# Local and strided scores in shared PSUM pairs, with a new order of operations

## The chip, the cores and the metric

The kernel runs on one core of one Trainium2 chip. The metric is the device time of one execution in microseconds; before the change it was 312.59 us (median of three runs, 310.74 to 312.9).

## The reference

A sparse attention over 8 batches, 8 heads, 576 positions and 64 dimensions per head, and behind it a feed-forward layer with ELU. All inputs and the output are float32.

```python
scores = q @ k^T / sqrt(64)
rel = pos[:, None] - pos[None, :]
mask_local   = (rel >= 0) & (rel < 32)                 # heads 0..3
mask_strided = (rel >= 0) & (pos[None] % 32 == pos[:, None] % 32)   # heads 4..7
attn = softmax(where(mask, scores, -1e9)) @ v
x = attn.transpose(0, 2, 1, 3).reshape(8 * 576, 512)
h = x @ w_in                                           # w_in 512 x 2048
g = where(h > 0, h, exp(min(h, 0)) - 1)
out = g @ w_out                                        # w_out 2048 x 512
```

## The kernel before

**Tokens of a sequence** are taken in 8 classes modulo 8, 72 positions each (`NS`, `RS`). A strided head then needs only positions of its own classes, so its scores are small blocks of 72 by 72; a local head needs, for each window of 96 positions (`LQ`), 128 keys. Heads are worked on in pairs: a key such as `3s1` is batch 3, strided (`s`) or local (`l`), pair 1 (`y`). Each pair is done in two halves (`u`).

**Attention, one half of a pair**: `S` computes the scores into two PSUM banks of 288 columns each (`scores`, L464: six local or eight strided matmuls of 64 rows, alternating between the banks), `e` takes the exp on ScalarE for both banks at once (`exp_s`, L471, 576 elements per partition), `m` multiplies by the 0/1 mask on VectorE (`mask`, L478 and L484), `O` multiplies by v and by ones, which gives the output and the sums of the exps (`pv`, L527 strided, L534 local; batches 0 and 1 in an older form with 64-column matmuls), `n` and `r` take Ln and Exp(-) of the sums on ScalarE (L562, L568), and `x` writes the product into `xT` (L593). Batches 0 to 2 are loaded plainly and transposed on TensorE (`T`, L418 and L421) with copies out of PSUM on VectorE (`c`) or ScalarE (`C`); for batches 3 to 7 the transposition is a DMA on SP's queue (`X`).

**Feed-forward**: 9 chunks of 512 tokens. Layer 1 has 16 blocks `m` per chunk, each four matmuls of 512 columns (`L`; in chunk 0 as `a`, inputs 2 and 3, the strided heads, and `b`, inputs 0 and 1, the local heads; L623). `h` is the exp of h on ScalarE (L631), `i` clamps it on VectorE (L640) or `j` on ScalarE (L638), `g` takes the maximum with h on VectorE (L651, after `j` L649). Layer 2 has four blocks `kk` of 128 tokens, each in four parts of four matmuls (`Z`, L657). `o` (ScalarE) or `q` (VectorE) copies a block to SBUF (L663) into one of four rotating `osb` tiles, and `t` stores it in two or three pieces from SP's queue (L675). The very last block is done in two halves of 256 columns (`Y`, L683, and `y`: the second half is copied by ScalarE and VectorE and stored by SP and ScalarE).

**Loads** (`D`) are issued by POOL: q, k, v by class (`qs`, `ks`, `ql`, ...; with two heads per load for batch 0), `wi0` to `wi3` and `wj0` for w_in (`wi0` and `wj0` half a quarter each) and `wo0` to `wo3` for w_out. The q and k of the first strided pair of batch 0 come by SP and ScalarE's queues into a staging tile. The other loads of batch 0 stand in the program ahead of the order. `V` copies the v rows that two windows share; `W` copies the strided v into a layout with ones between.

**What sets the order**: the string `ORDER`. It is gone through token by token, and each engine's queue is the sub-sequence of the tokens that it executes; PSUM banks are the digits at the end of a token (`S.3s0.1.56` uses banks 5 and 6). Semaphores keep readers behind writers, and a writer of a bank or of a rotating tile behind its last reader, a store's landing included. Within one engine nothing overtakes.

```python
    for tok in ORDER.split():
        f, *a = tok.split(".")
        run[f](*a)
```

Of the kernel before, what the change touches and what calls it, by code (L numbers as in the profile page):

```python
# [9 lines left out]
BF16 = mybir.dt.bfloat16  # L10
I32 = mybir.dt.int32
ALU = mybir.AluOpType
# [3 lines left out]
S = 576  # L16
D = 64
# [19 lines left out]
T.0s0.k.0.1 S.0s0.0.12 c.0s0.k.1 T.0s0.q.3.1 e.0s0.0 c.0s0.q.1 S.0s0.1.67 m.0s0.0 T.0s1.q.0 e.0s0.1  # L37
O.0s0.0.12 c.0s1.q m.0s0.1 T.0s1.k.7 n.0s0.0 F.ml D.wi0.0 O.0s0.1.56 r.0s0.0 c.0s1.k x.0s0.0 D.wj0.0
n.0s0.1 S.0s1.0.34 r.0s0.1 T.0l0.q.7 D.wi1.0 e.0s1.0 x.0s0.1 S.0s1.1.01 c.0l0.q T.0l0.k.2 e.0s1.1
D.wi2.0 m.0s1.0 c.0l0.k O.0s1.0.67 D.wi3.0 m.0s1.1 n.0s1.0 S.0l0.0.01 S.0l0.1.23 D.qs.1 V.0.0  # L40
e.0l0.0 O.0s1.1.45 e.0l0.1 D.ks.1 m.0l0.0 T.0l1.k.0 r.0s1.0 m.0l0.1 O.0l0.0.23 n.0s1.1 x.0s1.0
# [3 lines left out]
b.0.0 h.0.4 b.0.2 h.0.0 i.0.4 a.0.5.7 D.wo0.0 h.0.2 a.0.6.3 i.0.0 g.0.4 b.0.6 j.0.2 b.0.5 g.0.0  # L45
h.0.6 a.0.11.6 h.0.5 g.0.2 b.0.11 j.0.6 a.0.8.4 i.0.5 D.wo1.0 h.0.11 b.0.1 g.0.5 a.0.9.5 h.0.1 g.0.6
b.0.8 j.0.11 D.wo2.0 i.0.1 b.0.9 h.0.8 g.0.1 a.0.7.7 h.0.9 a.0.14.3 i.0.8 T.1s0.q.0 g.0.11 j.0.9
D.wo3.0 b.0.7 g.0.8 T.1s1.q.2 h.0.7 a.0.3.6 c.1s1.q T.1s0.k.1 C.1s0.q a.0.15.4 g.0.9 D.qs.2 C.1s0.k
T.1s1.k.2 i.0.7 b.0.15 c.1s1.k S.1s0.1.01 h.0.15 g.0.7 b.0.3 D.ks.2 e.1s0.1 b.0.14 i.0.15 h.0.3
g.0.15 T.1l1.q.7 S.1s0.0.01 h.0.14 m.1s0.1 S.1s1.0.45 D.ql.2 e.1s0.0 i.0.3 a.0.12.2 i.0.14 b.0.12  # L50
e.1s1.0 m.1s0.0 T.1l0.q.0 g.0.14 h.0.12 T.1l0.k.1 O.1s0.0.45 D.kl.2 C.1l0.q m.1s1.0 a.0.10.3 i.0.12
n.1s0.0 g.0.3 T.1l1.k.0 r.1s0.0 b.0.10 C.1l1.k x.1s0.0 a.0.13.6 g.0.12 h.0.10 O.1s0.1.45 C.1l0.k
c.1l1.q b.0.13 D.vs.2 V.1 n.1s0.1 S.1l1.0.12 h.0.13 Z.0.2.0.7 i.0.10 e.1l1.0 g.0.10 Z.0.1.0.0
r.1s0.1 m.1l1.0 j.0.13 x.1s0.1 S.1l0.1.12 g.0.13 O.1l1.0.34 D.vl.2 e.1l0.1 Z.0.2.1.7 n.1l1.0 m.1l0.1
r.1l1.0 Z.0.1.1.0 x.1l1.0 S.1l0.0.12 S.1s1.1.34 S.1l1.1.56 e.1l0.0 Z.0.2.2.7 e.1l1.1 m.1l0.0
Z.0.1.2.0 e.1s1.1 m.1l1.1 O.1l1.1.56 O.1l0.0.34 n.1l1.1 O.1s1.0.12 n.1l0.0 Z.0.2.3.7 m.1s1.1 n.1s1.0
r.1l0.0 r.1l1.1 Z.0.1.3.0 x.1l0.0 o.0.2 x.1l1.1 r.1s1.0 Z.0.0.0.3 t.0.2 o.0.1 x.1s1.0 Z.0.0.1.3
t.0.1 Z.0.0.2.3 Z.0.0.3.3 O.1s1.1.12 o.0.0 O.1l0.1.67 n.1s1.1 T.2s1.q.0 t.0.0 T.2s1.k.3 n.1l0.1
c.2s1.q r.1s1.1 T.2l0.k.5 c.2s1.k T.2l0.q.4 r.1l0.1 T.2l1.k.0 x.1s1.1 C.2l0.k T.2l1.q.3 x.1l0.1
S.2s1.0.12 C.2l1.k W.2 T.2s0.q.5 L.1.13.6 e.2s1.0 D.qs.3 c.2s0.q C.2l1.q c.2l0.q T.2s0.k.7 m.2s1.0  # L60
L.1.6.5 h.1.13 D.ks.3 V.2 j.1.13 c.2s0.k L.1.11.4 D.vs.3 h.1.6 g.1.13 D.ql.3 S.2s0.0.23 i.1.6 h.1.11
S.2l0.1.01 L.1.10.6 g.1.6 e.2s0.0 X.qs.3 i.1.11 e.2l0.1 L.1.8.7 m.2s0.0 h.1.10 g.1.11 O.2s0.0.01
h.1.8 L.1.5.2 m.2l0.1 i.1.10 n.2s0.0 i.1.8 O.2s1.0.34 X.ks.3 Z.0.3.0.5 g.1.10 r.2s0.0 g.1.8 h.1.5
Z.0.3.1.5 x.2s0.0 n.2s1.0 L.1.4.7 r.2s1.0 i.1.5 D.kl.3 g.1.5 L.1.7.6 h.1.4 x.2s1.0 Z.0.3.2.5 h.1.7
i.1.4 L.1.1.4 i.1.7 g.1.4 L.1.0.3 g.1.7 h.1.1 i.1.1 L.1.12.7 h.1.0 g.1.1 D.vl.3 X.ql.3 L.1.2.6 i.1.0
h.1.12 g.1.0 L.1.14.4 h.1.2 i.1.12 g.1.12 j.1.2 L.1.15.3 D.qs.4 h.1.14 g.1.2 L.1.3.7 h.1.15 i.1.14
g.1.14 j.1.15 S.2l1.1.12 Z.0.3.3.5 e.2l1.1 X.kl.3 g.1.15 h.1.3 m.2l1.1 S.2l1.0.01 S.2s0.1.23 o.0.3
L.1.9.4 i.1.3 e.2s0.1 g.1.3 D.ks.4 t.0.3 O.2l1.1.56 e.2l1.0 m.2s0.1 Z.1.0.0.7 h.1.9 m.2l1.0 n.2l1.1
# [84 lines left out]
def kernel(  # L153
# [597 lines left out]
```

## Time and profile before

| What | Value |
|---|---|
| runs | 312.59, 310.74, 312.9 us |
| profiled execution: span | 309.4 us (no separate time is listed for it) |
| TensorE busy | 297.2 us, 96% |
| ScalarE busy | 233.7 us, 76% |
| VectorE busy | 223.4 us, 72% |
| POOL busy | 74.8 us, 24% |
| granted TensorE clock, mean | 0.977 |
| first layer-1 matmul | at 18.38 us |
| first layer-2 matmul | at 39.44 us |
| end of the last matmul | 305.47 us |

How to read it: the span goes from the first to the last instruction of the profiled execution. Busy is the union of an engine's instructions; matmuls are pipelined, so a row's mean duration (381 ns for a 512-column matmul) is longer than the distance between two starts (216 ns). A row of a group reads: line, engine, operation, tiles, shapes, number of instructions, busy time, mean duration of one, and behind the bar the engine's idle time ahead of them and what ended it. "issue" is time in which the engine waited for nothing that the profile shows. The clock is a share of full speed, by slices of 7.7 us in the head of the page.

### The profile page before, as it was taken

Reading aid. Unit: us, or ns where it says so; the run is one execution under the profiler, and the core shown is the slowest. Engines: PE = TensorE matmul, PEld = TensorE weight load, DVE = VectorE, ACT = ScalarE, POOL = GpSimd, SP = SyncE. Lnnn points to the kernel's source line nnn. Section 1 sums busy time; section 2 is a strip of 40 time slices with the busy share of each in tenths; the row PEclk is TensorE's granted clock in tenths of the full one; section 3 lists DMA queues with packets and bytes.
Section 4 is the critical chain, followed back from the end, with each engine's and each line's share of the span. In section 5 each row is a group of like instructions: output and inputs, shape, how many; then the busy total and the mean of one; then the engine's idle time right before and its main releaser. Section 6 shows DMA issues by size and latency. Waiting matters only on the chain.

```text
span 309.4 us, 6379 instructions
## 1 busy us (share of the span) xinstructions
PE 297.2 (96%) x2374; PEld 151.6 (49%) x2412; DVE 223.4 (72%) x445; ACT 233.7 (76%) x410; POOL 74.8 (24%) x104
## 2 busy tenths in 40 slices
PE   5989999999999999999999999999999999999994
PEld 5754545544554455444544544455444544444443
DVE  6869972999669976898689679946798359990100
ACT  4769976979887899887998997879886767881211
POOL 8933310761084048003810082000000000000000
PEclk9559999999999999999999999999999999999999
DMA  8999999999999999994999589222200220002222
GB/s 161 189 206 206 195 206 213 165 133 152 151 200 161 123 201 183 106 125 87 190 155 122 119 113 159 47 67 71 68 3 0 70 68 1 0 2 57 67 79 70
DMA packets 96952, 36.29 MB, mean 117 GB/s; under 512 B 77754, under 2 KB 92442, under 8 KB 96922
## 3 DMA queue, kind: packets, MB, share of 16 engines
q0 software_dynamic: 64608, 19.40, 61.0%
q1 hardware_dynamic: 31878, 16.09, 28.9%
q10 hardware_dynamic: 436, 0.40, 0.5%
q8 instruction: 19, 0.31, 0.4%
q14 instruction: 11, 0.09, 0.1%
HBM read 39.41 MB, written 9.44 MB: 158 GB/s over the span
## 4 chain that ended last, share of the span: by engine, by line
PE 72%; DVE 15%; DMA 6%; issue 4%; ACT 2%; DVEq 0%; ACTq 0%
PE ps L657 34%; PE ps L623 27%; DVE g L651 6%; DMA vl<-in_v_dram 5%; DVE he L640 5%; PE ps L464 3%; PE ps L527 2%; PE ps L534 2%; DVE xT L593 1%; DMA g<-in_k_dram 1%; DVE g L649 1%; PE ps L683 1%; PE ps L421 1%; PE ps L418 1%; ACT he L631 1%
## 5 line engine op out<-in xcount | busy, mean ns | idle before, releaser
L623 PE MATMUL ps<-xT,w_in_sb 128*128 128x512 bf16 x560 | 129.6, 381 | 1.5 <-DVE g L651 0.4
L657 PE MATMUL ps<-w_out_sb,g 128*128 128x512 bf16 x538 | 128.9, 379 | 1.8 <-issue 1.0
L631 ACT ACTIVATE he<-ps 128x512 f32<-128x512 f32 x144 | 84.5, 594 | 23.3 <-PE ps L623 21.0
L623 PEld LDWEIGHTS <-w_in_sb 128*128 128x128 bf16 x576 | 55.1, 98 | 65.3 <-issue 2.3
L657 PEld LDWEIGHTS <-g 128*128 128x128 bf16 x560 | 50.6, 98 | 53.4
L651 DVE TENSOR_TENSOR g<-he,ps 128x512 bf16<-128x512 bf16 x112 | 74.0, 681 | 1.5
L640 DVE TENSOR_SCALAR he<-he 128x512 bf16<-128x512 f32 x112 | 46.3, 431 | 16.2 <-ACT he L631 15.7
L593 DVE TENSOR_TENSOR xT<-ps,ln 64x576 bf16<-64x576 f32 (+1 forms) x64 | 42.4, 678 | 21.6 <-ACT ln L568 21.1
L471 ACT ACTIVATE e<-ps 128x576 bf16<-128x576 f32 (+1 forms) x64 | 39.4, 646 | 5.8 <-PE ps L464 5.0
L562 ACT ACTIVATE ln<-ps 64x576 f32<-64x576 f32 (+1 forms) x64 | 36.3, 584 | 5.8 <-PE ps L527 2.6
L568 ACT ACTIVATE ln<-ln 64x576 f32<-64x576 f32 (+1 forms) x64 | 38.7, 620 | 1.4
L663 ACT COPY osb<-ps 128x512 f32<-128x512 f32 x27 | 15.8, 585 | 29.1 <-PE ps L657 26.1
L232 POOL DMA_DIRECT2D vs<-in_v_dram x8 | 5.3, 662 | 71.7 <-DVE vsp L603 69.4
L478 DVE TENSOR_TENSOR pm<-e,mask_s 72x576 bf16<-72x576 bf16 x32 | 14.4, 451 | 11.3 <-ACT e L471 10.8
L649 DVE SCALAR_TENSOR_TENSOR g<-he,ps 128x512 bf16<-128x512 bf16 x32 | 21.7, 680 | 0.6
L638 ACT ACTIVATE he<-he 128x512 bf16<-128x512 f32 x32 | 20.1, 627 | 0.7
L484 DVE TENSOR_TENSOR pm<-e,mask_l 128x576 bf16<-128x576 bf16 x32 | 14.5, 456 | 5.4 <-ACT e L471 4.4
L238 POOL DMA_DIRECT2D ql<-in_q_dram x20 | 16.3, 821 | 0.5 <-issue 0.4
L245 POOL DMA_DIRECT2D kl<-in_k_dram x20 | 15.5, 801 | 1.2 <-DMA vs<-in_v_dram 0.9
L527 PEld LDWEIGHTS <-vsp 72*128 72x128 bf16 x192 | 9.1, 98 | 5.8 <-DVE vsp L603 0.7
L700 DVE COPY osb<-ps 128x128 f32<-128x128 f32 x1 | 0.3, 291 | 15.0 <-ACT osb L699 15.0
L534 PEld LDWEIGHTS <-vl 128*128 128x128 bf16 x144 | 8.2, 97 | 4.4
(87 smaller groups left out, 176.4 us busy)
## 6 DMA issues: line engine op xcount, KB each, us to landing
out_dram<-osb SPq DMA_DIRECT2D x31, 144.0 KB
w_out_sb<-in_moe_w_out_dram POOLq DMA_DIRECT2D x4, 512.0 KB, 15.4
vl<-in_v_dram POOLq DMA_DIRECT2D x7, 288.0 KB, 6.6
qs<-in_q_dram POOLq DMA_DIRECT2D x5, 320.0 KB, 9.5
ks<-in_k_dram POOLq DMA_DIRECT2D x5, 320.0 KB, 11.2
vs<-in_v_dram POOLq DMA_DIRECT2D x5, 320.0 KB, 6.0
w_in_sb<-in_moe_w_in_dram POOLq DMA_DIRECT2D x3, 512.0 KB, 11.2
ql<-in_q_dram POOLq DMA_DIRECT2D x20, 72.0 KB, 6.9
```

What stands on the lines that cost most here:

```text
L238: nc.gpsimd.dma_start(out=t[0:RS, h % 2, :, h // 2, :], in_=q[b, h].rearrange("(p s) d -> p s d", s=NS))
L471: nc.scalar.activation(e[0:R], tiles.pop(("S", key, u))[0:R], ACT.Exp, scale=scale)
L562: nc.scalar.activation(t, s_ps, ACT.Ln)
L568: nc.scalar.activation(t, t, ACT.Exp, scale=-1.0)
L593: nc.vector.tensor_mul(dst, o_ps, rc)
L623: nc.tensor.matmul(tiles["h", ch, m], lhsT=w_in_sb[:, c, m * 128:(m + 1) * 128], rhs=xT[:, c, ch * CHUNK:(ch + 1) * CHUNK], start=(c == 2) ...
L631: nc.scalar.activation(e, tiles["h", i[0], i[1]], ACT.Exp)
L638: nc.scalar.activation(e1, e, ACT.Relu, bias=1.0, scale=-1.0)
L640: eng.tensor_scalar(e1, e, scalar1=1.0, scalar2=1.0, op0=ALU.min, op1=ALU.subtract)
L649: nc.vector.scalar_tensor_tensor(dst, e1, -1.0, h, op0=ALU.mult, op1=ALU.max)
L651: nc.vector.tensor_tensor(dst, e1, h, op=ALU.max)
L657: nc.tensor.matmul(ops, lhsT=g[ch % 2][:, m, kk * 128:(kk + 1) * 128], rhs=w_out_sb[:, m, :], start=(m == 0), stop=(m == MC - 1), skip_gro ...
```

## The change

For batches 3 to 7 the scores of a half of a local pair and three of the four strided blocks of a half of a strided pair share a pair of banks of 504 columns (`PW`: 288 local, 3 x 72 strided). The fourth strided blocks of all four halves share one pair of banks of 288 columns (`j` = 4). So a batch has five tokens `P`, five exps and five masks, where it had eight of each. The mask comes from one tile `mask_x` with the strided mask three times behind the local one. `O` picks its parts from these tiles; the masked tiles live until both local and strided `O` have read them. The loads of batch 0 and two mask selects become tokens of the order, and the whole order is made anew: sequence, banks, which clamps are `i` or `j` (112 and 32 before, 87 and 57 after), which output copies are `o` or `q` (27 and 8 before, 16 and 19 after), and the places of the loads, transposing DMAs and stores. Of the order, the beginning up to the first layer-1 tokens, one packed stretch and the end are shown.

```diff
+PACK = (3, 4, 5, 6, 7)
+PW = W + 3 * RS
...
-w.7.28 F.k1 F.vs k.k.0 k.q.0 T.0s0.k.0.0 F.ms C.0s0.k.0 T.0s0.q.1.0 K.q.1 k.k.1 c.0s0.q.0
...
-D.vs.1 T.0l1.q.1 r.0s1.1 c.0l1.k O.0l0.1.67 n.0l0.0 r.0l0.0 c.0l1.q n.0l0.1 V.0.1 D.ql.1 S.0l1.1.01
-x.0l0.0 r.0l0.1 x.0s1.1 e.0l1.1 S.0l1.0.23 x.0l0.1 a.0.0.4 e.0l1.0 m.0l1.1 D.kl.1 O.0l1.1.67 m.0l1.0
-O.0l1.0.23 n.0l1.1 r.0l1.1 a.0.2.5 n.0l1.0 x.0l1.1 a.0.1.0 r.0l1.0 D.vl.1 x.0l1.0 a.0.4.6 b.0.4
...
-Z.8.0.2.1 Z.8.0.3.1 Z.8.1.0.0 o.8.0 Z.8.1.1.0 t.8.0 Z.8.1.2.0 Z.8.1.3.0 o.8.1 t.8.1 Y.8.3.0.1
-y.8.3.0 Y.8.3.1.2 y.8.3.1
+F.k1 D.qs1.0 D.ks1.0 F.ms w.7.28 k.k.0 T.0s0.k.0.0 K.q.1 k.q.0 T.0s0.q.3.0 T.0s0.q.7.1 F.vs
+T.0s1.q.6 T.0s1.k.1 k.k.1 D.vs0.0 T.0s0.k.5.1 c.0s0.q.0 c.0s1.q c.0s1.k C.0s0.k.0 C.0s0.q.1
+S.0s0.0.67 e.0s0.0 D.ql0.0 D.kl0.0 S.0s1.0.01 D.vl0.0 F.m1 c.0s0.k.1 S.0s0.1.23 D.vs1.0 e.0s1.0
...
+F.ml e.0l0.1 e.0l0.0 O.0s1.0.01 V.0.0 m.0l0.1 r.0s0.1 T.0l1.q.3 D.ks.1 c.0l1.q n.0s1.0 O.0l0.1.67
+x.0s0.1 C.0l1.k O.0s1.1.23 r.0s1.0 n.0l0.1 D.qs.1 S.0l1.1.45 x.0s1.0 T.1s0.k.0 r.0l0.1 T.1s0.q.1
+n.0s1.1 r.0s1.1 x.0l0.1 T.1s1.q.7 e.0l1.1 C.1s0.k x.0s1.1 c.1s0.q m.0l0.0 m.0l1.1 D.vl1.0 S.0l1.0.23
+V.0.1 D.wi1.0 S.1s0.0.01 e.0l1.0 m.0l1.0 D.qs.2 O.0l0.0.56 D.wi2.0 e.1s0.0 m.1s0.0 O.0l1.1.34
+n.0l0.0 n.0l1.1 O.0l1.0.01 a.0.7.2 r.0l0.0 x.0l0.0 a.0.4.5 r.0l1.1 x.0l1.1 T.1s1.k.6 a.0.5.3 D.wi0.0
+c.1s1.q D.vs.1 n.0l1.0 r.0l1.0 x.0l1.0 b.0.5 b.0.7 D.wi3.0 h.0.7 c.1s1.k i.0.7 S.1s0.1.67 b.0.4
...
+P.3.3.12 e.3p.3 t.1.1 P.3.4.34 D.qs.5 L.2.0.0 e.3p.2 h.2.0 m.3p.3 L.2.8.7 h.2.8 L.2.6.1 e.3p.4
...
+L.8.13.1 h.8.13 i.8.13 g.8.13 Z.8.1.0.4 q.7.1 Z.8.1.1.4 Z.8.2.2.0 t.7.2 Z.8.2.3.0 Z.8.1.2.4
+Z.8.1.3.4 Y.8.3.0.5 t.7.3 Z.8.0.1.6 Z.8.0.2.6 t.7.1 q.8.1 Z.8.0.3.6 q.8.2 t.8.2 q.7.0 t.7.0 t.8.1
+y.8.3.0 q.8.0 t.8.0 Y.8.3.1.7 y.8.3.1
...
+    p_pm4 = ctx.enter_context(tc.tile_pool(name="p_pm4", bufs=2)) if PACK else None
...
-    mask_l = consts.tile([128, 2, NS, 3, LN], BF16, tag="mask_l", name="mask_l")
+    mask_x = consts.tile([128, 2, PW if PACK else W], BF16, tag="mask_x", name="mask_x")
+    mask_l = mask_x[:, :, 0:W].rearrange("p u (s b n) -> p u s b n", s=NS, b=3)
...
+        elif b == 0:
+            y = int(what[2])
+            if nm == "vl":
+                load_vpair(0, y)
+            else:
+                load_runs(nm, 0, 2 * y, 2)
...
-    load_runs("vs", 0, 0, 2)
-    load_runs("qs", 0, 2, 2)
-    load_runs("ks", 0, 2, 2)
-    load_runs("vs", 0, 2, 2)
...
-    for y in range(2):
-        load_runs("ql", 0, 2 * y, 2)
-        load_runs("kl", 0, 2 * y, 2)
-        load_vpair(0, y)
...
+        elif what == "mx":
+            mx = mask_x[:, :, W:]
+            nc.vector.memset(mx, 0.0)
+            for u in range(2):
+                nc.vector.tensor_copy(mx[0:RS, u].rearrange("p (i n) -> p i n", n=RS),
+                                      mask_s.unsqueeze(1).to_broadcast([RS, 3, RS]))
...
+    def scores_packed(b, j, bk):
+        i0, i1, j = int(bk[0]), int(bk[1]), int(j)
+        sc = tiles["S", b + "p", j] = ps[:, i0:i1 + 1:i1 - i0, 0:PW if j < 4 else W]
+        items = ([("l", j // 2, j % 2, i) for i in range(3)] + [("s", j // 2, j % 2, i) for i in range(3)]
+                 if j < 4 else [("s", k // 2, k % 2, 3) for k in range(4)])
+        c0 = 0 if j == 4 else W
+        for c, y, u, i in items:
+            P = Pair(f"{b}{c}{y}")
+            for z in range(2):
...
+                nc.tensor.matmul(dst, lhsT=P.kT[pr, k0:k0 + 128], rhs=rhs, start=True, stop=True,
+                                 skip_group_check=True)
+            if P.str:
+                c0 += RS
+
+    def exp_packed(key, j):
+        j = int(j)
+        R, n = (128, PW) if j < 4 else (RS, W)
+        e = tiles["e", key, j] = p_e.tile([128, 2, PW], BF16, tag="e", name="e")
+        nc.scalar.activation(e[0:R, :, 0:n], tiles.pop(("S", key, j))[0:R], ACT.Exp, scale=scale)
+
+    def mask_packed(key, j):
...
+            pm = p_pm.tile([128, 2, PW], BF16, tag="pm", name="pm")
+            nc.vector.tensor_mul(pm, e, mask_x[:, j % 2].unsqueeze(1).to_broadcast([128, 2, PW]))
+        tiles["pm", key, j] = pm
...
+        def part(z, i):
+            if not P.str:
+                return local_cols(pm[:, z, 0:W], i)
+            if P.b in PACK and i == 3:
+                return pm4[:, z, k * RS:(k + 1) * RS]
+            return pm[0:RS, z, c0 + i * RS:c0 + (i + 1) * RS]
```

More of the change, by code (lines that the diff above doesn't have):

```diff
@@ L541, in pv @@
         P, u = Pair(key), int(u)
-        pm = tiles.pop(("pm", key, u))
+        if P.b in PACK:
+            k = 2 * P.y + u
+            pm, pm4 = (tiles["pm", key[0] + "p", i] for i in (k, 4)) if P.str else (
+                tiles["pm", key[0] + "p", k], None)
+            c0 = W
+        else:
+            pm, c0 = tiles.pop(("pm", key, u)), 0
+        def part(z, i):
[4 more added lines that the diff above has]
+            return pm[0:RS, z, c0 + i * RS:c0 + (i + 1) * RS]
         if not P.old:
             ov = banks(bk)
-            pv_new(P, pm, u, ov)
+            pv_new(P, part, u, ov)
             ys = slice(P.y * D, (P.y + 1) * D)
@@ L706 @@
         "f": lambda *a: fill(*a, nc.scalar.copy),
+        "P": scores_packed,
         "c": lambda *a: copy_T(nc.vector.tensor_copy, *a),
         "C": lambda *a: copy_T(nc.scalar.copy, *a),
[L709 removed]
+        "S": scores, "O": pv,
+        "e": lambda key, u: (exp_packed if key[1] == "p" else exp_s)(key, u),
+        "m": lambda key, u: (mask_packed if key[1] == "p" else mask)(key, u), "n": log_sums, "r": recip, "x": write_x,
         "V": copy_vloc, "W": copy_vstr, "D": load, "X": dma_T,
```

256 lines of the change are left out of this document (134 added, 122 removed).

## The prediction

> **What bounds the kernel now.** I read the page's head first, then engine time by stretch, the costliest groups, the list of waits, and last the timelines of the start and the end.
>
> ```profile
> span 309.4 us, 6379 instructions
> PE 297.2 (96%) x2374; PEld 151.6 (49%) x2412; DVE 223.4 (72%) x445; ACT 233.7 (76%) x410; POOL 74.8 (24%) x104
> ...
> PEclk9559999999999999999999999999999999999999
> ```
>
> TensorE is busy nearly always; only slices 2 and 3 show half the clock. The same by stretch (columns: length; busy time of PE, weight load, DVE, ACT, POOL; clock; DMA share; GB/s):
>
> ```profile
> 0.00:20.44 20.44, 15.77 (x254) 12.71 (x255) 15.38 (x50) 13.36 (x27) 14.84 (x28) 0.70 1.23 183
> 20.44:40.00 19.56, 19.15 (x210) 9.65 (x212) 16.81 (x36) 17.19 (x35) 7.37 (x10) 0.96 1.36 201
> 40.00:290.00 250.00, 246.90 (x1829) 120.89 (x1861) 190.11 (x358) 200.21 (x344) 52.58 (x66) 1.00 0.90 108
> ...
> 305.47:309.40 3.93, 0.00 (x0) 0.00 (x0) 0.29 (x1) 0.27 (x1) 0.00 (x0) 0.92 0.16 49
> ```
>
> From 40 to 290 us TensorE idles 3.1 us in all. Whatever the change does to ScalarE and VectorE there, it cannot win more than these 3.1 us plus what it takes out of TensorE's own stream. What else can move is the start (until the chunks flow) and the last 3.93 us, in which no matmul runs.
>
> **The packed scores, counted.** Per batch 3 to 7, eight score blocks of two banks by 288 columns become four of 504 (local 288 plus three strided blocks of 72) and one of 288. The matmuls stay: 24 local and 32 strided before, 4 x 12 + 8 after. Exps and masks fall from 8 to 5.
>
> ```profile
> L471 ACT ACTIVATE e<-ps 128x576 bf16<-128x576 f32 x32 | 20.1, 647 | 3.0 <-PE ps L464 2.5
> L562 ACT ACTIVATE ln<-ps 64x576 f32<-64x576 f32 x48 | 30.0, 642 | 3.5 <-PE ps L527 2.6 <-PE ps L534 0.2
> L562 ACT ACTIVATE ln<-ps 128x288 f32<-128x288 f32 x16 | 6.2, 411 | 2.3 <-PE ps L507 1.2 <-PE ps L491 1.1
> L484 DVE TENSOR_TENSOR pm<-e,mask_l 128x576 bf16<-128x576 bf16 x32 | 14.5, 456 | 5.4 <-ACT e L471 4.4
> ```
>
> No row has 1008 elements. From 411 ns at 288 and 642 at 576, an element costs 0.80 ns and an instruction 180; so 1008 elements take about 0.99 us, and a batch's exps 4 x 0.99 + 0.65 = 4.6 instead of 5.2 us: 2.7 us of ScalarE for five batches. Bounds: one instruction no cheaper than 0.65, no dearer than the two that it replaces, 1.29; at 1.29 ScalarE gains nothing. VectorE saves about as much, 2 us, by the same reasoning from 456 ns. On the path both are worth nothing while TensorE is full. They are also spent again: the new order moves 25 clamps from VectorE (431 ns) to ScalarE (627) and 11 output copies from ScalarE (585) to VectorE (689), which leaves ScalarE some 6 us heavier.
>
> **Mode changes, the one gain in TensorE's stream.** The list of waits has this line:
>
> ```profile
> PEld L464 <- issue: 12.3, 30, 0.6
> ```
>
> Thirty times the weight load stood still about 0.41 us ahead of scores, waiting for nothing shown. TensorE itself feels less: a 512-column matmul is followed by its like after 216 ns, by scores after 311; and the last score matmul before a full-size one takes about 130 instead of about 40. So each change costs 0.09 us. Counted along both orders, changes between 128-row, 64-row and 64-column matmuls fall from 92 to 74: **-1.6 us** (bounds -0.9 if only leaving or entering costs, -2.2). The Trainium skill, TensorEngine Tiling, "Key Properties", says that a change of tiling mode drains TensorE; the row agrees, and it speaks for this part.
>
> **The body of the order.** By TensorE time between tokens (0.216 us per 512-column matmul), a layer-1 bank is reused after 4.9 us (median) where it was 3.5, and from scores to their PV in batches 3 to 7 lie 13.9 us (least 3.8) where it was 3.2 (least 1.5). Exp, mask and the queue ahead of them hide easily. Against that stands one stretch, some 165 to 180 us along TensorE's work, where ScalarE's work back to back (0.49 us an exp of h, 0.54 a clamp, 0.93 a packed exp) is 1.1 times TensorE's: up to 1.5 us of delay; the longer bank reuse covers most. For loads, each first packed block of a batch has its transposing DMA at least some 10 us earlier, though it now needs local and strided operands together. I take **+0.3** (bounds -2 and +3).
>
> **The start.** Loads land in order of issue: half loads of 160 KB at 6.60, 7.38, 8.23, then every 0.8 to 0.9 us; 320 KB in 1.6, 1 MB of weights (512 KB here) in 2.5. The new queue puts q and k of the second strided pair first, and ahead of the last v half and the first weights it puts k and q of batch 1. By these steps the last v half lands at 17.4 (14.17 before), w_in's second quarter at 19.9; chunk 0 now starts there, with m = 7, 4, 5. That would do, since the first layer-1 matmul ran at 18.38. But TensorE's queue also has batch 1's three strided transposes (0.62 us each at half clock) ahead of the scores 0l1.0, and all the rest of batch 0 hangs on those. Walking the three queues with the rows: first exp 8.8 (VectorE fills vs_p, 0.95 us, ahead of the first copy; it was 7.46); S.0l1.1 at 17.4 (17.14 before); transposes 17.9 to 19.7; S.0l1.0 at 19.8 (18.02); its exp to 20.5 and mask to 21.4, behind V.0.1; PV until 22.8; Ln, Exp and product until 24.35. So layer 1 can go on with inputs 0 and 1 at 24.4, where it did at 22.08. In TensorE work at warm prices, 14.9 us are then done against 14.4, so the start is **+2.0** behind. Cover: the batch 1 work pulled ahead is not lost, it is in the 14.9. Two edits cost nothing: the two mask selects on POOL (0.33 and 0.31 us) now stand between batch 0's loads, but POOL issues a load in 0.6 us while one lands in 0.8, and without that lead each would delay the later landings by its 0.3; the new fill of the joint mask, about 0.8 us on VectorE, falls where VectorE has 15% to spare and nothing in batch 2 reads it.
>
> Then the clock, by the windows in which it was granted:
>
> ```profile
> 8.37:11.79 3.42, 3.42 (x66) 2.76 (x68) 2.58 (x9) 2.71 (x6) 3.35 (x7) 0.50 1.57 189
> 11.79:15.20 3.41, 3.25 (x72) 2.69 (x68) 2.95 (x7) 2.42 (x6) 3.08 (x5) 0.50 1.69 185
> 15.20:18.61 3.41, 2.73 (x52) 2.20 (x48) 3.31 (x9) 3.23 (x10) 1.27 (x2) 0.50 1.29 204
> 18.61:22.03 3.42, 3.06 (x21) 1.44 (x21) 1.81 (x5) 2.11 (x5) 1.18 (x1) 0.50 1.25 208
> 22.03:25.44 3.41, 3.41 (x17) 1.57 (x16) 1.55 (x4) 2.27 (x5) 0.76 (x1) 1.00 1.24 206
> ```
>
> Busy with transposes and small blocks, TensorE stayed at 0.50; full clock came after the window with five 512-column matmuls. In the new order these begin at about 22.8, a window later, so the clock may return at 25.4: six matmuls at 0.43 instead of 0.216 us, +1.3. I take +0.7 between 0 and 1.3: the start is **+2.7** (bounds -1, if the weights' landing alone sets it, and +4). The Trainium skill, TensorE: Matmul & The Clock Gate, "Part 4: PE-mode transpose", says that transposes do not count as busy for the clock; by it the later window is right and the sum would be 0.6 higher. The windows agree as far as they go.
>
> **The end.** Before, each output tile had its store long ahead:
>
> ```profile
> 301.81 3.66 PE L683 MATMUL ps<-w_out_sb,g 128*128 128x256 bf16 x32
> 303.80 0.37 ACT L696 COPY osb<-ps 128x256 f32<-128x256 f32 x1 [1.16 <-PE ps L683]
> 305.50 0.27 ACT L699 COPY osb<-ps 128x128 f32<-128x128 f32 x1 [1.33 <-PE ps L683]
> 305.80 0.29 DVE L700 COPY osb<-ps 128x128 f32<-128x128 f32 x1 [14.96 <-ACT osb L699]
> 306.12 0.65 ACTq L675 DMA_DIRECT2D out_dram<-osb  x1
> ```
>
> After the last matmul (305.47): copies, issue at 306.12, landing at 308.09, end. Four osb tiles rotate. In the new order q.8.0, on VectorE, takes the tile of q.8.1, and t.8.1 stands on SP behind t.8.2 and t.7.0; and y.8.3.1's VectorE copy is queued behind q.8.0, its SP store behind t.8.0. With E the end of the last matmul: q.8.1, q.8.2, q.7.0 until E-4; t.8.2, t.7.0, t.8.1 (three pieces each at 0.37) until E-1.2; t.8.1 lands 1.5 later, E+0.3; q.8.0 until E+1.1; t.8.0 until E+2.2; y.8.3.1's store at E+2.3 to 2.6, where it was E+0.65. That is **+2.2** with landings at 0.2 to 0.5 slower (bounds 0, if the wait does not bind, and +3).
>
> ```profile
> ACT osb L663 <- DMA out_dram<-osb: 2.9, 1, 2.9
> ```
>
> That such a copy does wait for the store of its tile is seen once already.
>
> **Sum**, against the profiled execution's span: 2.7 + 2.2 - 1.6 + 0.3 = **+3.6 us**, 309.4 to 313.0. The three runs lie 1.3 to 3.5 us above that span, median 312.59; so the forecast is **316.2**, 1.2% slower; own range 314.3 to 318.2.
>
> **Rivals.**
> 1. *Not slower: the start fills.* If O.0l1.0 ends by 20 us, layer 1 starts as w_in lands, and batch 1's work already done counts in full: start -1.0, sum -0.1, 312.5. For it: ScalarE is busy 13.36 of 20.44 us, there is room. Against: the transposes at half clock. It decides at a start of layer 1's second half before 21.5 us.
> 2. *The tail does not bind*: +1.4, 314.0. For it: stores end 1.4 us after issue in places; against, VectorE's and SP's order.
> 3. *ScalarE becomes the bound* at 155 to 195 us: the surplus of 1.5 us shows in full and a second stretch near 75 to 90 (0.98) adds 0.8: 318.5. Against: bank reuse of 4.9 us.
> 4. *Faster by over 1%*: rivals 1 and 2 together and 2 us of the 3.1 idle us gone: 308.3.
> 5. *The change does not do what it says*: packed exps at 1.29 us free nothing; ScalarE is then 1.5 us per two batches fuller and rival 3 gets likelier, up to 319.
>
> **Chances.** Forecast 0.47, rival 1 0.18, 2 0.12, 3 0.12, 4 0.05, 5 0.06. A measurement of this kernel tells about 1% (3.1 us) from no change. Slower by over that (above 315.7): 0.33 of the forecast's 0.47, rivals 3 and 5, and 0.04 of 2 with a worse start: 0.55. Faster 0.05; within 1% 0.40. The range runs from rival 1 with a little more to rivals 3 and 5: 311.5 to 320.
>
> **What would show it.** Start: first L471 at about 8.8, second half of layer 1 near 24.4, clock 1.00 from 22.0 or 25.4. Packed: L471's new form of 1008 elements near 0.99 us, x20, and the mask near 0.68. Mode changes: fewer than 30 stops of PEld before scores. Body: TensorE idle at most 4 us between 45 and 290. End: a VectorE copy to osb waiting for a DMA, and some 6 us between the last matmul and the end. I am wrong if layer 1 starts before 20 us, if the end stays at 4 us, or if TensorE has stretches with ScalarE full in the middle.

## The result, and the profile after

The changed kernel takes 313.34 us (median of 13 runs, 312.81 to 315.34), the kernel before 311.83 (13 runs, 310.74 to 313.63): ratio 1.0055, 95% interval 1.0039 to 1.007. So it is slower by 1.5 to 1.7 us, where 3.6 were forecast.

The page's head, and engine time by stretch:

```profile
span 313.5 us, 6289 instructions
PE 300.6 (96%) x2373; PEld 153.9 (49%) x2412; DVE 226.1 (72%) x420; ACT 236.7 (75%) x408; POOL 74.5 (24%) x104
```

```profile
0.00:20.44 20.44, 17.22 (x284) 14.41 (x284) 14.85 (x49) 14.11 (x30) 14.87 (x28) 1.00 1.18 184
20.44:40.00 19.56, 18.25 (x196) 8.79 (x197) 15.20 (x32) 14.13 (x30) 7.50 (x10) 1.00 1.39 200
40.00:290.00 250.00, 246.21 (x1801) 120.73 (x1834) 190.44 (x332) 207.25 (x348) 52.16 (x66) 1.00 0.82 106
309.05:313.50 4.45, 0.00 (x0) 0.00 (x0) 0.29 (x1) 0.27 (x1) 0.00 (x0) 1.00 0.40 119
```

In the middle TensorE idles 3.8 us (3.1 before), ScalarE is busy 7 us more, and 4.45 us lie behind the last matmul (3.93). The clock column reads 1.00 at the start only because records of the clock are missing there; the distance of the matmuls shows half clock until 27.4 us (below).

**Two things about the numbers come first.** Each of the 13 runs lists its time and its span; they differ by 1.66 to 1.81 us. So the execution of before with span 309.4 stands for some 311.1 us, 0.7 under its median, and that of after (313.5, time 315.25) lies 1.9 above its median. The two profiles are 4.1 us apart, the medians 1.5: about 2.5 us of what the profiles show between them belongs to these two executions and not to the kernels.

To see where, I set up an account that doesn't depend on matmul records (38 or 39 are missing in each of these two traces, no weight load is): TensorE's work is every weight load's matmul at its undisturbed price (0.216 us for 512 columns; 288.6 us in all, in both kernels), and the **lag** is the time minus the work done by then.

| us | before | after | difference | forecast |
|---|---|---|---|---|
| lag at 40 us (start) | 10.9 | 13.3 | +2.4 | +2.7 |
| added from 40 us to the last matmul (body) | 6.0 | 7.2 | +1.2 | -1.6 + 0.3 |
| last matmul to end | 4.0 | 4.5 | +0.5 | +2.2 |
| sum | 20.9 | 25.0 | +4.1 | +3.6 |

The sum of the forecast nearly meets that of these two executions, by errors that cancel: that is luck. The row of the body is no accident of the two. From the weight load that runs at 45.2 us in *after* to the end of the last matmul, four traces with this body (*after*, *start_both*, *tail*, *fill_after*, see below) take 263.5 to 263.9 us; from the load at 45.05 us in *before*, three traces with the body of before (*before*, *fill_early*, *fill_all*) take 259.8 to 260.4. (The two stretches hold different work, so only the scatter within each is to be compared.) The new instructions themselves, shapes kept apart:

```profile
L504 ACT ACTIVATE e<-ps 128x1008 bf16<-128x1008 f32 x20 | 19.6, 1006 | 2.5 <-PE ps L495 1.6 <-DVE pm L517 0.9
L517 DVE TENSOR_TENSOR pm<-e,mask_x 128x1008 bf16<-128x1008 bf16 x20 | 13.6, 680 | 5.0 <-ACT e L504 4.8
L504 ACT ACTIVATE e<-ps 72x576 bf16<-72x576 f32 x5 | 3.2, 641 | 1.3 <-PE ps L495 1.3
```

1.006 us for the exp of 1008 elements and 0.68 for its mask, as worked out; the change does what it says. In the list of waits (each line: microseconds in total, times, longest) the stops of the weight load ahead of scores (two lines now) fall from 30 to 23, and those ahead of layer 1, which I read as a bank that isn't free yet, rise; before they were 2.3 us, 9 times:

```profile
PEld L495 <- issue: 5.5, 13, 0.4
PEld L689 <- issue: 5.2, 17, 0.5
PEld L468 <- issue: 4.4, 10, 0.8
```

That second line turned out to be the main one. The end, in order of time:

```profile
304.32 6.02 SPq L741 DMA_DIRECT2D out_dram<-osb  x15
304.75 0.37 ACT L762 COPY osb<-ps 128x256 f32<-128x256 f32 x1 [6.33 <-PE ps L749]
307.34 0.69 DVE L729 COPY osb<-ps 128x512 f32<-128x512 f32 x1 [2.45 <-PE ps L723]
309.38 0.29 DVE L766 COPY osb<-ps 128x128 f32<-128x128 f32 x1 [1.35 <-DMA out_dram<-osb]
309.70 0.57 ACTq L741 DMA_DIRECT2D out_dram<-osb  x1
```

The copy at 307.34 (q.8.0) waited for its own matmuls (PE) and for no store. By the semaphores that it waits on, it took the tile of q.8.2, whose stores are the first three of the 15 (304.32 to 305.43). The stores of q.8.1, whose tile the forecast gave it, were still being issued (306.76 to 307.92) when it began. The last copy, at 309.38, ran right behind ScalarE's (309.08 to 309.35), as before. What remains is SP's queue of 15 issues, which runs until 310.34, 1.3 us past the last matmul. Before, it was 1.0:

```profile
299.21 7.23 SPq L675 DMA_DIRECT2D out_dram<-osb  x9
```

The DMA packets agree. Before, the last packet of the output belongs to ScalarE's store (2.27 us past the last matmul; SP's 2.01); after, to SP's (2.85; ScalarE's 2.68).

### The profile page after: what moved, and what is told of

Read it like the earlier page. It is cut to its first block, busy times and chain, and to the rows that moved or that the text cites. A ratio compares the mean times of both kernels' runs of the same rounds, so it can differ in the third digit from the quotient of the medians.

```text
span 313.5 us, 6289 instructions
## 1 busy us (share of the span) xinstructions
PE 300.6 (96%) x2373; PEld 153.9 (49%) x2412; DVE 226.1 (72%) x420; ACT 236.7 (75%) x408; POOL 74.5 (24%) x104
## 4 chain that ended last, share of the span: by engine, by line
PE 65%; DVE 10%; ACT 9%; DMA 5%; issue 4%; POOL 3%; SPq 1%; ACTq 0%; DVEq 0%
PE ps L723 31%; PE ps L689 29%; ACT he L697 4%; DMA w_in_sb<-in_moe_w_in_dram 3%; DVE g L717 3%; DVE he L706 3%; ACT ln L628 2%; DMA out_dram<-osb 2%; PE ps L495 2%; DVE xT L659 1%; PE ps L586 1%; PE ps L579 1%; DVE g L715 1%; ACT he L704 1%; ACT ln L634 1%
## 5 line engine op out<-in xcount | busy, mean ns | idle before, releaser
L689 PE MATMUL ps<-xT,w_in_sb 128*128 128x512 bf16 x558 | 138.7, 384 | 3.2 <-DMA w_in_sb<-in_moe_w_in_dram 0.9
L717 DVE TENSOR_TENSOR g<-he,ps 128x512 bf16<-128x512 bf16 x87 | 59.0, 684 | 2.2
L706 DVE TENSOR_SCALAR he<-he 128x512 bf16<-128x512 f32 x87 | 38.5, 449 | 19.9 <-ACT he L697 19.2
L715 DVE SCALAR_TENSOR_TENSOR g<-he,ps 128x512 bf16<-128x512 bf16 x57 | 38.3, 683 | 16.6 <-ACT he L704 16.5
L704 ACT ACTIVATE he<-he 128x512 bf16<-128x512 f32 x57 | 35.5, 628 | 1.3
L504 ACT ACTIVATE e<-ps 128x1008 bf16<-128x1008 f32 (+1 forms) x25 | 22.6, 933 | 3.8 <-PE ps L495 2.9
L729 DVE COPY osb<-ps 128x512 f32<-128x512 f32 x19 | 12.8, 685 | 10.7 <-PE ps L723 10.6
L524 ACT ACTIVATE e<-ps 72x576 bf16<-72x576 f32 (+1 forms) x24 | 15.1, 648 | 4.5 <-PE ps L468 2.8
L517 DVE TENSOR_TENSOR pm<-e,mask_x 128x1008 bf16<-128x1008 bf16 x20 | 13.6, 680 | 5.0 <-ACT e L504 4.8
L255 POOL DMA_DIRECT2D vl<-in_v_dram x7 | 8.4, 1204 | 11.2 <-PE ps L586 9.2
```

The costliest lines, as they stand in the source:

```text
L504: nc.scalar.activation(e[0:R, :, 0:n], tiles.pop(("S", key, j))[0:R], ACT.Exp, scale=scale)
L689: nc.tensor.matmul(tiles["h", ch, m], lhsT=w_in_sb[:, c, m * 128:(m + 1) * 128], rhs=xT[:, c, ch * CHUNK:(ch + 1) * CHUNK], start=(c == 2) ...
L704: nc.scalar.activation(e1, e, ACT.Relu, bias=1.0, scale=-1.0)
L706: eng.tensor_scalar(e1, e, scalar1=1.0, scalar2=1.0, op0=ALU.min, op1=ALU.subtract)
L715: nc.vector.scalar_tensor_tensor(dst, e1, -1.0, h, op0=ALU.mult, op1=ALU.max)
L717: nc.vector.tensor_tensor(dst, e1, h, op=ALU.max)
```

## Experiments

All ratios are to the kernel before, run on the same chip. The changed kernel itself was run only with the first result, so a difference to it goes from one comparison to another; the medians of the kernel before in these lie between 311.69 and 312.14 us. Where a row speaks of waits, it is for 40 to 300 us: the distance of two matmul starts over the first one's price, less about 0.1 us where the shape changes to or from 64 rows, by what ended it.

**The start.** *start_both* undoes it in two points:

```diff
-... T.0l1.q.3 D.ks.1 ... D.qs.1 S.0l1.1.45 x.0s1.0 T.1s0.k.0 r.0l0.1 T.1s0.q.1 ... D.vl1.0 ... D.wi1.0 S.1s0.0.01 ...
+... T.0l1.q.3 D.vl1.0 D.wi1.0 D.ks.1 ... D.qs.1 S.0l1.1.45 x.0s1.0 r.0l0.1 ...
+... a.0.7.2 ... a.0.4.5 ... a.0.5.3 ... b.0.5 b.0.7 ... T.1s0.k.0 ... T.1s0.q.1 ... S.1s0.0.01 ...
```

> The changed kernel with its start undone in two points: the last v half of batch 0 and w_in's second quarter are issued ahead of batch 1's k and q, and batch 1's strided transposes and first scores stand behind the first three layer-1 blocks. If the start makes the changed kernel slower (the profiles show it 2.6 us behind at 30 us), the first layer-1 matmul comes near 19 us (21.52 in the changed kernel, 18.38 before), the clock returns a window earlier, and 1.5 to 2.5 us are won: 0.998 to 1.001 of before. Rival: the start of the profiled execution was only unlucky and the extra time comes from the body of the order: the ratio stays at 1.0055 within 0.0015.

Measured: 313.72 us, 1.0061 [1.0039, 1.0084]. The start begins as was asked for (first full-size matmul recorded at 19.94, distance 0.216 from 20.80), and the time is that of the changed kernel. But what it gains it gives back: the transposes that were put off leave no full-size matmul between 22.79 and 25.22 us, and the weight load at 45.2 us of *after* comes at 43.16, in the middle of the ten profiles compared below. So this run alone doesn't show that the start costs nothing. Why the profile said otherwise shows in other kernels with the unchanged start. The changed kernel first, then *two_exps* (below), whose start is the same:

```profile
21.52 1.49 PE L689 MATMUL ps<-xT,w_in_sb 128*128 128x512 bf16 x3 [0.88 <-DMA w_in_sb<-in_moe_w_in_dram]
22.80 0.69 PE L422 MATMUL ps<-identity,xT 72*128 72x72 bf16 x8
23.30 2.75 PE L689 MATMUL ps<-xT,w_in_sb 128*128 128x512 bf16 x6
```

```profile
21.09 1.49 PE L692 MATMUL ps<-xT,w_in_sb 128*128 128x512 bf16 x3 [0.35 <-issue]
22.37 0.69 PE L422 MATMUL ps<-identity,xT 72*128 72x72 bf16 x8
22.86 1.55 PE L692 MATMUL ps<-xT,w_in_sb 128*128 128x512 bf16 x6
```

Six matmuls in 2.75 us or in 1.55: the same queue, at half and at full clock. Ten profiles share this start (after, and the kernels below except where start, fillers or queues differ early). Full clock (the first full-size matmul that its like follows within 0.23 us) is back between 22.38 and 27.52 us in them, and the start goes with it. TensorE's queue is the same in all ten up to there, so the same weight load can be compared, the one at 40.0 us in *after*: it comes 1.7 to 2.55 us earlier in the seven where the clock was back by 24 us, and 1.0, 0.2 and 0 us earlier where it came at 25.8, 26.0 and 27.5. As a lag that is 10.75 to 11.6, 12.3, 13.1 and 13.3. Three profiles with the start of before have 10.8, 10.9 and 11.7. Median against median, some 11.3 and 10.9: the new start costs a few tenths at most, and the profiled execution of after was its worst case. The Trainium skill, TensorE: Matmul & The Clock Gate, "What's actually happening", has the clock come back after about 3.4 us of sustained work, watched in free-running windows. The scatter agrees with that in kind; its 5.1 us are more than one such window, and why is not shown.

**Does the clock decide the start?** *fill_early*, *fill_all* (on the kernel before) and *fill_after* (on the changed one) put filler matmuls into the start:

```diff
+T.0s0.k.0.0 w.7.8 ... T.0s0.q.1.0 w.7.8 ... T.0s0.k.0.1 w.7.8 S.0s0.0.12 w.7.8 ... T.0s0.q.3.1 w.7.8   # fill_early
+... S.0s0.1.67 w.7.3 ... T.0s1.q.0 w.7.3 ... O.0s0.0.12 w.7.3 ...   # and so on to layer 1: fill_all, fill_after
```

> The kernel before with eight filler matmuls of 128 columns on a zero tile (as its own warm-up does) behind each of the first five blocks of transposes and scores, 40 x 0.056 us at full clock, in gaps of TensorE of 0.2 to 0.5 us. In the kernel before the clock falls to 0.50 at 8.37 us, after a window with 1.7 us of work in 3.4. If that window decides, the clock stays up for at least one window more, and 0.5 to 1 us is won: 0.997 to 0.9985 of before. Rival: the fillers only delay what follows: 1.000 to 1.004.

> As fill_early, and three more fillers behind every block of transposes, scores and O up to the first layer-1 block (19 x 3 x 0.056 = 3.2 us at full clock, 6.1 at half). If the clock stays up until layer 1, the start is bound by the landing of w_in and by the other engines, and 1 to 2.5 us are won: 0.992 to 0.997. Rival: it falls all the same and the fillers cost their 6 us at half clock, or half of that: 1.008 to 1.02.

> The changed kernel with the fillers of fill_all in its own start. If the clock decides its start: 1.5 to 3 us won on it, 0.996 to 1.001 of before, and a narrower spread of times. Rival: 1.014 or more.

Measured: 1.0027 [1.0002, 1.0053], 1.0096 [1.0058, 1.0133], 1.0178 [1.0148, 1.0208]. In *fill_all* the clock stayed at 1.00 from 8.94 us on, as the windows show (and two neighbouring fillers, mostly 0.055 to 0.061 us apart from there, 0.107 before):

```profile
15.20:18.60 3.40, 2.96 (x63) 2.25 (x61) 2.58 (x6) 1.70 (x4) 1.28 (x2) 1.00 1.29 205
18.60:22.00 3.40, 3.40 (x80) 2.52 (x79) 2.60 (x7) 2.48 (x6) 1.18 (x1) 1.00 1.24 207
```

and yet the first full-size matmul came at 23.16 (18.38 before), and the weight load at 45.05 us of *before* came at 48.85. The fillers kept the clock and delayed the chain from scores to products by more than that was worth. A start held at full clock can't be had this way; and since the fillers changed the chain too, the effect of the clock alone remains a reading of ten profiles.

**The packing by itself.** *pack_alone* keeps the order of before:

```diff
-S.5s0.0.12 ... e.5s0.0 ... m.5s0.0 ... S.5l0.0.01 ... e.5l0.0 ... m.5l0.0
+P.5.0.12 P.5.4.34 ... e.5p.0 e.5p.4 ... m.5p.0 m.5p.4   # batches 3, 4, 6, 7 in the same way
```

> The packing alone, in the order of before: each P takes the place and the banks of the earlier of the two score tokens that it replaces, the fourth strided blocks a free pair of banks close by; start, loads, clamps, copies and end are those of before. Changes of matmul shape along TensorE's queue fall from 93 to 77. If a change costs TensorE 0.09 us and the saved exps and masks lie off its path, 1.4 us are won: ratio 0.9955 to before. Rival: the joint blocks ask for four operands at once and hold their masked tiles longer, which costs what the changes save: 1.000 or above, and then the extra time of the changed kernel comes from the packing and not from its start.

Measured: 1.0481 [1.0438, 1.0524]: 15 us slower, the rival's side and far past it. The shape changes fell as forecast (1.8 us less in the body), but TensorE waits 16.0 us: for transposing DMAs of k (5.6), for exps (3.5), for maxima (2.9), for masks (1.7).

```profile
PEld L495 <- DMA kTl<-kl: 5.2, 2, 3.4
PE ps L495 <- DMA kTl<-kl: 4.2, 2, 2.9
```

A joint block needs local and strided operands at once, and at the earlier of the two places one of them hasn't landed. In this form, with the joint block at the earlier place, the packing can't live in the old order.

**The price of a shape change.** *split_p* adds 24 of them:

```diff
-P.3.3.12 e.3p.3 t.1.1 P.3.4.34 D.qs.5 L.2.0.0
+P.3.3.12.0 t.1.1 P.3.4.34 D.qs.5 L.2.0.0 P.3.3.12.1 e.3p.3   # .0: eight matmuls, .1: the other four
```

> The changed kernel with each of the twenty blocks of 504 columns computed in two parts (eight matmuls and four) with the next full-size token of TensorE's queue between them; the exp follows the second part. Changes of matmul shape rise from 75 to 99, nothing else is added. At 0.09 us a change: 2.2 us slower than the changed kernel, 1.0125 of before. If TensorE feels only the entering half (0.095 for every second change): 1.1 us, 1.009. Rival: the stops of the weight load are hidden and cost nothing: 1.0055.

Measured: 321.82 us, 1.0316 [1.0281, 1.035], 8.5 us above the changed kernel and not 2.2. The trace parts it: the 70 changes of the body cost 7.2 us, 0.103 each (46 cost 4.8 in the changed kernel, 0.104; 56 cost 5.9 before, 0.105), so the 24 cost 2.4. The rest are waits, 7.9 us instead of 3.8 (together 6.5 of the 6.75 us between the two profiles), half of the rise for the packed exps, which come one TensorE token later. The price of the step was right; what a delay of some 0.9 us (a token of four full-size matmuls) to twenty exps does was not in it.

**ScalarE and VectorE.** *two_exps* takes the saved instructions back:

```diff
-nc.scalar.activation(e[0:R, :, 0:n], tiles.pop(("S", key, j))[0:R], ACT.Exp, scale=scale)
+for z in range(2):
+    nc.scalar.activation(e[0:R, z, 0:n], sc[0:R, z], ACT.Exp, scale=scale)   # the mask likewise
```

> The changed kernel with every packed exp and every packed mask done as two instructions, one for each bank: 25 more instructions on ScalarE (about 0.18 us each, 4.5 us in all) and 20 more on VectorE. If what the packing saves on these engines is worth nothing because TensorE is full, the time stays that of the changed kernel: 1.0055 within 0.0015. Rival: ScalarE is the bound in a stretch of the middle: 1 to 2 us more, 1.009 to 1.012.

Measured: 314.11 us, 1.008 [1.0056, 1.0105]; 0.8 us above the changed kernel, intervals overlapping: unclear, at most a small price. (Time and span differ by 2.0 to 2.1 us in its runs, 0.3 more than in the changed kernel's, so within the span it is 0.5.) *copies_act* and *clamps_back* move work between the engines:

```diff
-q.2.0 q.2.3 q.2.2 q.3.0 ...   # 13 copies of chunks 2 to 6, VectorE
+o.2.0 o.2.3 o.2.2 o.3.0 ...   # copies_act: ScalarE
-... j (57 on ScalarE), i (87 on VectorE)
+... j (32), i (112), each clamp where it was before   # clamps_back
```

> The changed kernel with the thirteen output copies of chunks 2 to 6 that VectorE makes given back to ScalarE (585 ns there, 689 on VectorE). If VectorE is late because of these copies, its waits shrink and 0.5 to 1.5 us are won: 1.001 to 1.004 of before. Rival: ScalarE, busy over 80% in the body, becomes late instead: 1.006 or more.

> The changed kernel with each clamp on the engine that did it before: 32 on ScalarE instead of 57, 112 on VectorE instead of 87. VectorE gets about 25 x 0.44 = 11 us more in all, ScalarE 25 x 0.63 = 16 us less. If the clamps that were moved make ScalarE late and TensorE wait, 0.5 to 1.5 us are won: 1.001 to 1.004 of before. If VectorE is the one that is late (without its clamps the kernel took 0.9978 of before, without ScalarE's 1.0012), it gets slower: 1.008 or more.

Measured: 322.4 us, 1.0315 [1.0274, 1.0356], and 332.0 us, 1.0626 [1.059, 1.0662]. Neither helps; 7.6 us more on ScalarE cost 9, some 11 more on VectorE cost 19. In *copies_act* two waits of TensorE, 2.0 and 3.3 us, make up most of it. Ahead of the first, ScalarE stands idle in front of a copy whose matmuls aren't done, with other work behind it:

```profile
158.14 0.59 ACT L729 COPY osb<-ps 128x512 f32<-128x512 f32 x1 [1.95 <-PE ps L723]
```

The stops ahead of layer 1 in *clamps_back*:

```profile
PEld L689 <- issue: 14.4, 34, 2.0
```

So in this order the clamps and copies can't simply go back. The two runs mix two things, though: the load of an engine, and places in its queue that were chosen for the other one. Whether an order made for the old division would do better is not shown. Then all clamps away, from both kernels, and from one engine at a time (the exps of h then live until the maximum, so they get five buffers instead of four):

```diff
-    p_he = ctx.enter_context(tc.tile_pool(name="p_he", bufs=4))
+    p_he = ctx.enter_context(tc.tile_pool(name="p_he", bufs=5))
+        if True:   # after_no_j: eng is nc.scalar; after_no_i: eng is nc.vector
+            tiles["he1", i] = (e, eng is nc.scalar)
+            return
         e1 = p_he1.tile([128, CHUNK], BF16, tag="he1", name="he1")
```

> The changed kernel without its clamps (all 144, i and j): the maximum takes the exp itself, so min and -1 of the ELU are left out. ScalarE loses 57 instructions of 0.63 us, VectorE 87 of 0.44, some 37 us each. If the body loses time because TensorE waits for these two engines (3.8 us between 40 and 300 us), the waits go and 3 to 3.5 us are won on the changed kernel: 0.995 of before, and about 1 us below the kernel before without clamps, since what is left is start (equal), changes of matmul shape (-1.1) and end (+0.5). Rival: the loss is not one of waits: 1 to 2 us above the kernel before without clamps.

> The kernel before without its clamps, in the same way (32 on ScalarE, 112 on VectorE). Its body shows 1.7 us of waits, so it can win 1 to 1.7 us: 0.995 to 0.997 of before under either theory. It is what the changed kernel without clamps is compared with.

> The changed kernel without the 57 clamps on ScalarE alone (min and -1 are left out there): 36 us less on ScalarE, nothing changed on VectorE. If ScalarE is what makes VectorE late (it hands over the exps and the Ln and Exp of the sums), nearly all of the 3 us is won: 0.996 of before. If VectorE is late by its own work, less than 1 us: 1.002 or more.

> The changed kernel without the 87 clamps on VectorE alone: 38 us less on VectorE, nothing changed on ScalarE. If VectorE is late by its own work, as the waits for g and xT are written in the trace, nearly all of the 3 us is won: 0.996 of before. If it is late because of ScalarE, less than 1 us: 1.002 or more.

| kernel | median us | ratio, interval | waits in the body | lag added in the body |
|---|---|---|---|---|
| before | 311.83 | | 1.7 | 6.0 |
| after | 313.34 | 1.0055 [1.0039, 1.007] | 3.8 | 7.2 |
| before_no_clamp | 310.43 | 0.995 [0.9932, 0.9967] | 0.8 | 4.9 |
| after_no_clamp | 310.49 | 0.9956 [0.9939, 0.9973] | 0.9 | 4.3 |
| after_no_j (ScalarE relieved) | 312.12 | 1.0012 [0.9992, 1.0032] | 2.2 | 6.1 |
| after_no_i (VectorE relieved) | 310.92 | 0.9978 [0.9959, 0.9997] | 1.4 | 5.2 |

The stops ahead of layer 1, without clamps, in the changed kernel and then in the kernel before:

```profile
PEld L689 <- issue: 1.9, 7, 0.3
```

```profile
PEld L623 <- issue: 1.0, 4, 0.3
```

With both engines relieved the two kernels take the same time (310.49 and 310.43): what puts the changed kernel behind goes away with the work on VectorE and ScalarE, and TensorE's waits go with it. VectorE counts more (2.4 us won against 1.2; 2.9 with both). Neither alone won nearly all of the 3 us, as each expectation had it for the case that its engine is the late one. Clamps are part of the chain that frees a bank, too, so these runs take away load and turnaround together and don't part the two. The expected lead of 1 us for the changed kernel without clamps did not appear: the body is 0.6 better instead of 1.1, and the end takes 0.3 back.

**Can the waits be mended?** *body_fix* moves the ten TensorE tokens that waited, and the mask fill; *tail* the end; *all_three* does both:

```diff
-... F.mx ... O.2l0.1.01 O.2s0.1.56 ... L.1.14.7 t.0.1 Z.1.2.0.2 ... L.3.0.1 L.3.11.4 ... L.6.0.1 ... Z.5.2.3.0 ...
+x.1l0.1 F.mx ... O.2s0.1.56 O.2l0.1.01 ... t.0.1 Z.1.2.0.2 L.1.14.7 ... L.3.11.4 L.3.0.1 ... Z.5.2.3.0 L.6.0.1 ...
-Y.8.3.0.5 t.7.3 Z.8.0.1.6 Z.8.0.2.6 t.7.1 q.8.1 Z.8.0.3.6 ... y.8.3.0 q.8.0 t.8.0 Y.8.3.1.7 y.8.3.1   # tail
+t.7.3 Z.8.0.1.6 Z.8.0.2.6 t.7.1 q.8.1 t.8.1 Z.8.0.3.6 ... q.8.0 Y.8.3.0.5 t.8.0 y.8.3.0 Y.8.3.1.7 y.8.3.1
```

> The changed kernel with the places mended where TensorE waits for VectorE between 45 and 290 us: ten tokens of TensorE's queue (seven layer-1 blocks and three O) stand one or two tokens later, so that the product or the maximum that frees their bank is done, and the fill of the joint mask moves from 74.5 us to about 50 us, where VectorE idles 1.7 us. Nothing is added or taken away. In the profile of the changed kernel the waits for g and for xT between 40 and 300 us sum to 3.1 us, before it was 1.1. If they are what makes the body slower, 1.5 to 2.5 us are won: 0.998 to 1.001 of before. Rival: the waits only move to the next token, because VectorE itself is late: 1.0055 within 0.0015.

> The changed kernel with its end put in the order of before: block 0 of the last chunk is done ahead of both halves of block 3, and its copy and store stand ahead of theirs, so that nothing but the two halves is left at the end. In the profiles 4.5 us lie between the last matmul and the end of the changed kernel, 4.0 before. If SP's queue of stores makes the difference: about 0.5 us won, 1.004 of before and 4.0 us at the end. Rival, the step of the forecast: 2.2 us won, 0.9985.

> The changed kernel with the tokens and the fill of body_fix and with the end of tail together. If the body's waits and the end make the changed kernel slower than before, both are gone: 2 to 3 us won, 0.996 to 0.999 of before, and what is left to its favour are the changes of matmul shape, 1.1 us in the body. Rival: 1.004 (the end alone).

Measured: 1.0068 [1.0047, 1.009], 1.0057 [1.0034, 1.0079], 1.0079 [1.0054, 1.0104]; none wins what was expected. In *body_fix* the waits for maxima fell from 2.1 to 0.4 us, those for products into xT rose from 1.0 to 2.5 and for exps from 0.3 to 0.9: they moved on, as the rival said. In *tail* the end grew to 5.0 us: SP has as many stores to issue and is done with them at 308.00, 1.8 us past the last matmul (306.24), where it was 1.3:

```profile
301.25 6.75 SPq L741 DMA_DIRECT2D out_dram<-osb  x14
```

The rival of *tail*, 2.2 us won, did not come either. In *all_three* neither part won anything.

*h_early* moves the queues of ScalarE and VectorE instead, and *h_early_cb* adds clamps_back to it:

```diff
-L.2.0.0 e.3p.2 h.2.0 m.3p.3 L.2.8.7 h.2.8 L.2.6.1 e.3p.4 L.2.12.6 m.3p.2 L.2.10.5 L.2.2.2 i.2.0 g.2.0 i.2.8
+L.2.0.0 e.3p.2 h.2.0 m.3p.3 L.2.8.7 i.2.0 h.2.8 L.2.6.1 i.2.8 g.2.0 e.3p.4 L.2.12.6 ...
```

> The changed kernel with the exp of h put right behind the TensorE token that follows its block, the clamp one TensorE token later and the maximum one more, wherever they stood later than that (chunks 1 to 8); TensorE's queue, the engines that do the work and all else are the same. From the last matmul of a block to the end of its maximum lie 3.97 us in the median (0.91 of them until the exp starts), before it was 2.85 (0.32). If this long turnaround is what makes TensorE wait, it falls to 3 us and 1 to 2 us are won: 0.999 to 1.002 of before. Rival: the two queues are only as full as they must be, and what the blocks win, the masks and products of attention lose: 1.0055 or more.

> The queues of h_early with the clamps of clamps_back. If the turnaround alone decides: like h_early within 0.002. If the balance of the two engines decides: apart from h_early by as much as clamps_back is from the changed kernel.

(In both, two maxima of the last chunk, 8.0 and 8.6, come ahead of blocks of chunk 6's layer 2 that still read their tile; those blocks use the newer data.) Measured: 336.51 us, 1.078 [1.0752, 1.0807], and 350.36, 1.1233 [1.1197, 1.127]. The turnaround did fall, by 0.9 to 1.0 us in the median, and the waits rose to 25 us, 12 of them for products into xT. What the blocks win, attention loses, and more. *h_early_cb* lies 0.045 above *h_early*, near the 0.057 that *clamps_back* adds to the changed kernel: the division of the work between the engines counts whatever the turnaround. No version here that does the whole work beats the kernel before.

## Why the prediction was right and wrong

**What came true, and what of it was luck.** Slower, by little, with TensorE full in the middle: right. Exp and mask at 0.99 and 0.68 us: 1.006 and 0.68. But the forecast had the loss come from the start (+2.7) and the end (+2.2), with the body and the shapes a gain of 1.3 together; in the runs most of it comes from the body. That the sign held is luck in good part. The sum was +3.6, the medians say +1.5.

**The steps that failed.** The start and the end were put 4 us too high together; that made the forecast too high. The body was put 1.8 us too low, and there the mechanism was missed that costs the changed kernel its time.

**The body.** It was put at +0.3, because a layer-1 bank is reused after 4.9 us where it was 3.5. But that distance is no slack until the turnaround is set against it: from the end of a block's last matmul to the end of its maximum lie 3.7 us in the median in the new order (a tenth of them over 7.8), 2.7 before (a tenth over 3.2). Of this rise 0.35 us is the exp of h, which starts 0.60 us behind its block instead of 0.25. (The expectation of *h_early* has 3.97, 2.85, 0.91 and 0.32, by a count from a slightly earlier point.) Waits rose from 1.7 to 3.8 us, 2.1 of these for maxima, 1.0 for products into xT, 0.3 for exps: **+2.1**. I had compared demand and capacity of ScalarE over long stretches (1.1 at worst) and found one place that might bind. What the trace has instead are short waits, most of 0.2 to 0.5 us, spread from 41 to 237 us; that rival 3 would show as a stretch at 155 to 195 us was wrong too, and VectorE is the nearer bound of the two. How much of the waits is load and how much the places in the two queues stays open: *h_early* shortened the turnaround and made them grow, *body_fix* only moved them. The step "on the path both are worth nothing while TensorE is full" was about the saved exps and masks, and for these *two_exps* bears it out to within 0.8 us.

**Shape changes.** Price right (0.09 forecast, 0.104 measured). The 18 fewer counted along the order are 10 in the body; the others fall into the start, where nothing of them shows. So -1.1 and not **-1.6**. The Trainium skill, TensorEngine Tiling (Array Packing), "Key Properties", says that changing the mode drains TensorE; three kernels here put that at 0.103 to 0.105 us a change.

**The start.** +2.7 met the profiled execution (+2.4), but not by its mechanism. The walk of the queues was too slow: S.0l1.1 at 17.4, in fact 15.5; S.0l1.0 at 19.8, in fact 18.2; the product that the second half of layer 1 needs at 24.35, in fact 22.4. That half (b.0.5) began at 24.1, close to the 24.4 forecast, but for other reasons: what held layer 1 in the profiled execution was the landing of w_in at 21.1, forecast for 19.9, and then the clock; in *two_exps*, where the clock came back sooner, b.0.5 began at 23.4. I took one execution's phase for the kernel's: in the median the start costs **0 to +0.4**, between the forecast and rival 1 (-1.0), whose sign, b.0.5 before 21.5 us, did not come.

**The end** was **+0.5** and not +2.2: q.8.0 took the tile of q.8.2, which was free, and not that of q.8.1, for whose store the forecast had it wait. Rival 2 named that outcome. The forecast's sign of being wrong, an end that stays at 4 us, nearly came: 4.5.

**The base.** I added the sum to the median of three runs, 312.59, though the profiled execution was a lower one. By the offset of 1.74 its time is 311.1, and 13 runs have the median 311.83: 0.8 us of the error of 2.9.

**Put together**, for typical executions: start 0 to +0.4, waits +2.1, shapes -1.1, end +0.5: +1.5 to +1.9, where the medians say +1.5. Most of these terms are read from single profiles, so agreement to a few tenths is as much as they can show.

## What to carry to other kernels

Where TensorE is full and two other engines are busy over 70%, a longer distance between the uses of a buffer says nothing until the turnaround of the buffer in the new order is set against it; read both from the same queue. One profile is one execution: before a difference in the start is put down to the change, compare it over several profiles, and bring spans to times with the offset that the runs list. An edit that joins two blocks also joins their inputs, so it is costed together with the order that it needs, not alone.

## What was not expected of the hardware

- The time at which full clock returned scattered by 5.1 us (22.38 to 27.52) for one and the same start, worth up to 2.55 us at the same weight load.
- Filler matmuls on a tile of zeros, with which TensorE was busy 2.6 to 3.4 us in windows of 3.4, kept the clock at 1.00 where it otherwise fell to 0.50 after a window with 1.7 us of work.
- Changes in the queues of ScalarE and VectorE cost far more than their own time: 25 clamps more on VectorE (11 us of work, at places that were made for ScalarE) 19 us, twenty exps 0.9 us later about 4 us of waits. A copy at a place that was made for the other engine held ScalarE idle for 1.95 us.
